# Causal attention and a gated MLP on one core: the score products of later pairs of heads in another number format

## The chip, the cores and the metric

The kernel runs on one core of one Trainium2 chip. The metric is the device time of one execution in microseconds. A core has a TensorE matrix engine (PE; its weight loads are listed apart as PEld), a vector engine (DVE), ScalarE (ACT), GpSimd (POOL) and SyncE (SP), whose queue issues all of this kernel's DMA transfers.

## What is computed

Causal attention over 4 batches of 12 heads (448 positions, 64 values a head), then a gated MLP over 768 channels with a mixing along the sequence. The reference, shortened:

```python
scores = q @ k.transpose(0, 1, 3, 2) / sqrt(64)
attn = softmax(where(causal, scores, -1e9))
x = (attn @ v).transpose(0, 2, 1, 3).reshape(4, 448, 768)
h = gelu_tanh(x @ w_in)
u, v = h[..., :512], h[..., 512:]
v_n = (v - mean(v)) / sqrt(var(v) + 1e-6) * g_ln
v_s = einsum('ts,bsd->btd', w_sg, v_n) + b_sg[None, :, None]
out = x + (u * v_s) @ w_out
```

All inputs and outputs are fp32.

## The kernel before

The work of a batch is six pairs of heads (24 pairs in all, `pair`, L475) and one MLP (`mlp`, L636). Two heads of a pair lie in the two halves of the 128 partitions, 64 rows each.

A pair loads q and k transposed, side by side, into one tile `qk` of 128x896 values (L481, L482; a pool of two such tiles). `score` (L485 to L491) multiplies them in fp32: four chunks of queries and keys (the table `CH`, L24), with 448, 64, 320 and 192 key columns, issued as two groups, (448, 64) and (320, 192). In each chunk the two heads stand one after the other in the code, on rows 0 to 63 and 64 to 127 of the array, into separate PSUM banks. The vector engine scales and masks the scores and takes the row minimum of the negated values (L503), ScalarE does exp with running sums (L511). The sums' reciprocals are transposed (L525), copied (L526), written to a scratch in memory (`rd`, L530) and read back as a broadcast tile `rb` (L533; two buffers, L524). TensorE transposes the probabilities (L542), ACT and DVE evict them into `ph` (L547, L549), `pv` multiplies them with v (L573), and DVE scales the result with `rb` into `xt` (L585). `keep_x` (L592) stores `xt` as the residual and splits it into a high part rounded to fp32r (L597 on POOL for batch 0, L599 on ACT later) and a low part, the difference (POOL, L600 and L602).

The MLP works with fp32r throughout: each product is the sum of three, high by high, high by low, low by high, with 128 rows of the array and 448 or 512 columns a matmul (`group`, L611 to L621, three matmuls of a group at a time). Its weights are split in the same way during the start (`split_w`, L407; `split_w64`, L420). The parts are: v half of the first product with GELU and normalisation (L646 to L688; the normalising step is L675), u half (L689), sequence mixing and gate (L702), output product (L730), which reads the residual from memory into `res` tiles of 128x2x448 (L737, L738, two buffers), adds it (L750) and stores the sums, two blocks of 128 channels together for batches 0 to 2 (L758) and singly for the last batch (L754).

The order is not that of the code. `Order` (L92) collects all steps with an engine, an estimated duration, their reads and writes and a priority (`at`), then places them one by one in a simulated schedule (`plan`, L136): on each engine, of the steps that are ready, the one with the lowest priority value goes first. Priorities come from `STEP`, `MLP` and `LEN` (L41 to L43) and from the offsets in `DUE` (L55). Durations are the estimates passed to `od.add`; they affect the order alone. A buffer's next use waits for all users of its previous one. Each engine runs its list in order, and a waiting step holds up all behind it; this holds for SP's transfers too.

Of the kernel before, what the change touches and what calls it, by code (L numbers as in the profile page):

```python
# [37 lines left out]
)  # L38
PW = 1024

STEP = [10.25, 12.58, 26.17, 15.7]  # L41
MLP = [-9.07, 44.62, 63.06, -36.56]
LEN = [120.74, 28.59, 116.13, 144.04]  # L43

EV = 10, 10, 10, 10

WARM, FILL, EARLY = 10, 0, 2

# [4 lines left out]
BANKS = dict(s=6, tx=1, ty=1, o=2, m=6)  # L53

DUE = dict(  # L55
    gb=-70.31, r=(-73.94, 167.17, -182.74, -112.01), load=(-22.24, -27.25, 21.84, 40.98),
    S=(-24.73, 16.46, -37.71, 59.93), mx=(-67.58, -177.74, -157.41, -61.27),
    ex=(-6.0, -124.31, 178.09, -22.45), inv=(-79.87, -84.21, -150.39, -0.57),
    Tr=(-30.25, -187.23, -175.59, 53.63), T=(-15.71, 12.99, -7.14, 20.55),
    ev=(-69.22, -68.97, -23.68, -241.47), V=(-34.92, 18.81, -178.88, -94.68),  # L60
    PV=(-7.79, -32.53, 14.54, 62.09), xo=(-147.05, 14.03, -41.95, -96.66),
    xs=(5.67, -159.72, 24.75, 158.69), post=(50.68, 88.74, -27.16, 37.5), wv=-22.34, wu=145.87,
    wo=100.49, mu=(6.77, 13.82, -8.74, 40.54), ms=(3.19, 41.66, -9.72, 72.98),
    mo=(-13.84, 150.66, 53.35, 188.48),
)
# [225 lines left out]
def attention_gated_mlp(ctx: ExitStack, tc: tile.TileContext, qk, vP, w_in, g_ln, w_sgT, b_sg, w_out, out):  # L291
# [53 lines left out]
    def dma(fn, r, w, at, size, early=0.0):  # L345
        od.add("sp", 0.48, fn, r, w, at, size=size / 330e3, early=early)
# [8 lines left out]
        od.add("dve", 0.068 + n * rate / 1000, fn, r, w, at, done, port=port)  # L355

    def pool_tt(n, fn, r, w, at):
        od.add("pool", 0.15 + n * 0.0021, fn, r, w, at, port=True)

    def start(p):  # L360
        b, h = divmod(p, HP)
# [58 lines left out]
    def split_w64(src, dst, key, n, at, pool_, tag, words, early=0.0):  # L420
        t = buf(pool_, tag, *words)
        it = lambda: t.t.bitcast(I32).rearrange("p a b -> p (a b)")[:, 0:2 * n].rearrange("p (n t) -> p n t", t=2)
        lo = lambda: it()[:, :, 0]
        hi = lambda: it()[:, :, 1]
        dma(lambda: nc.sync.dma_start(out=t.t.bitcast(I32).rearrange("p a b -> p (a b)")[:, 0:2 * n],
                                      in_=src.bitcast(I32)), [], [t], at - 6, n * 1024, early)
        kh, kl = (t, "hi"), (t, "lo")
        act(n, lambda: nc.scalar.activation(out=f(hi()), in_=f(hi()), func=AF.Prelu, scale=2.0 ** -112, alpha=2.0 ** 32),  # L428
            [t], [kh], at, True)
        dve(n, lambda: nc.vector.tensor_scalar(out=lo(), in0=lo(), scalar1=29, scalar2=None,  # L430
                                               op0=ALU.logical_shift_right), [t], [kl], at, 0.53, port=True)
        dve(n, lambda: nc.vector.scalar_tensor_tensor(out=lo(), in0=hi(), scalar=3, in1=lo(),
                                                      op0=ALU.logical_shift_left, op1=ALU.bitwise_or),
            [t, kh], [kl], at, port=True)
        od.add("pool", 0.13 + n * 0.0012, lambda: nc.gpsimd.tensor_copy(dst(0), f(lo())), [t, kl], [(key, 0)], at, port=True)
        pool_tt(n, lambda: nc.gpsimd.tensor_tensor(out=dst(1), in0=f(lo()), in1=f(dst(0)), op=ALU.subtract),
                [t, kl, (key, 0)], [(key, 1)], at)

# [9 lines left out]
    def weights_b():  # L448
        def load():
            nc.sync.dma_start(out=gcol, in_=g_ln)  # L450
            nc.sync.dma_start(out=bB, in_=bass.AP(tensor=b_sg.tensor, offset=b_sg.offset, ap=[[0, 128], [1, S]]))

        dma(load, [], ["gb"], 20, 229e3, LATER["g"])

        def halve():
            nc.vector.tensor_scalar(out=gcol, in0=gcol, scalar1=0.5, scalar2=None, op0=ALU.mult)
            nc.vector.tensor_scalar(out=bB, in0=bB, scalar1=0.5, scalar2=None, op0=ALU.mult)

        dve(512, halve, ["gb"], ["gb"], DUE["gb"])
# [15 lines left out]
    def pair(p):  # L475
# [2 lines left out]
        per = STEP[b]  # L478
        ib = [(2 * p + z) % NP for z in range(2)]
        s = [[bank("s") for k in range(2)] for z in range(2)]  # L480
        qk_ = buf(two, "qk", [128, 2, S])  # L481
        dma(lambda: nc.sync.dma_start(out=qk_.t, in_=qk[p]), [], [qk_], T + due("load", b), 459e3)  # L482


        def score(cs):  # L485
            for c in cs:
                m, n, bk, col, q0 = CH[c]
                for z in range(2):
                    r = slice(64 * z, 64 * z + 64)
                    nc.tensor.matmul(out=s[z][bk].t[:, col:col + n], lhsT=qk_.t[r, 0, q0:q0 + 128],  # L490
                                     rhs=qk_.t[r, 1, 0:n], start=True, stop=True)  # L491
        for cs in ((3, 0), (2, 1)):
            pe(sum(max(CH[c][1] * 4 / 2400, 0.214) + 0.01 for c in cs), lambda cs=cs: score(cs), [qk_],
               [s[z][CH[cs[0]][2]] for z in range(2)], T + due("S", b), (64, 128))


# [24 lines left out]
            nc.vector.tensor_reduce(out=tot, in_=sm[ip], op=ALU.add, axis=mybir.AxisListType.X)  # L521
            nc.vector.reciprocal(out=rs, in_=tot)
        od.add("dve", 0.3, inv, sk + ["sm"], ["rs"], T + due("inv", b))
        rb, sb = buf(two, "rb", [128, 512]), s[1][1]  # L524
        pe(0.12, lambda: nc.tensor.transpose(sb.t[0:8, 0:128], rs.rearrange("p z c -> p (z c)"), ident), ["rs", "ident"], [sb], T + due("Tr", b))  # L525
        dve(128, lambda: nc.vector.tensor_copy(rT[ip], sb.t[0:8, 0:128]), [sb], [("rT", ip)], T + due("inv", b))  # L526

# [64 lines left out]
    def keep_x(b, hp, x, To, Ty):  # L592
# [43 lines left out]
    def mlp(b):  # L636
# [93 lines left out]
        for mc in range(KC):  # L730
            ps = bank("m")
            at = step(2.27) + due("mo", b)
            d = slice(mc * 128, (mc + 1) * 128)
            z = mc % 2
            if z == 0:
                d2 = slice(mc * 128, (mc + 2) * 128)
                rr = buf(two, "res", [128, 2, S])  # L737
                dma(lambda rr=rr, d2=d2: nc.sync.dma_start(out=rr.t, in_=xd[b, d2, :].rearrange("(a p) s -> p a s", a=2)),  # L738
                    [("xd", b, mc), ("xd", b, mc + 1)], [rr], at - 6, 459e3)
            mms, r = [], []  # L740
            for c in range(FC):
                y = gT[c]
# [4 lines left out]

            cuts = ((0, S // 2), (S // 2, S)) if (b, mc) == (B - 1, KC - 1) else ((0, S),)
            for k, (lo, hi) in enumerate(cuts):
                dve(hi - lo, lambda rr=rr, ps=ps, z=z, lo=lo, hi=hi: nc.vector.tensor_tensor(  # L750
                    out=rr.t[:, z, lo:hi], in0=ps.t[:, lo:hi], in1=rr.t[:, z, lo:hi], op=ALU.add),
                    [ps, rr], [(rr, 2 * k + z)], at + 2.3 + due("post", b))
                if b == B - 1:
                    dma(lambda rr=rr, d=d, z=z, lo=lo, hi=hi: nc.sync.dma_start(out=out[b, d, lo:hi],  # L754
                                                                                in_=rr.t[:, z, lo:hi]),
                        [(rr, 2 * k + z)], [], at + 2.3, 512.0 * (hi - lo))
            if b < B - 1 and z:
                dma(lambda rr=rr, d2=d2: nc.sync.dma_start(out=out[b, d2, :].rearrange("(a p) s -> p a s", a=2),  # L758
                                                           in_=rr.t), [(rr, 0), (rr, 1)], [], at + 2.3, 459e3)
# [50 lines left out]
```

## Time and profile before

| | us |
|---|---|
| median of 3 runs (382.56 to 383.92) | 383.64 |
| profiled execution, its own time | 383.15 |
| its span, first to last instruction | 381.4 |
| PE busy | 372.1 |
| DVE busy | 255.3 |
| ACT busy | 211.8 |
| POOL busy | 146.6 |

The execution's own time is 1.75 us longer than the span. Busy time counts every stretch in which at least one instruction of the engine is under way; matmuls overlap, so a busy PE says that work is in its pipeline, not that it runs at its peak. A matmul's duration in the records contains a latency that the next one hides: the cost of one in a run is the distance between starts. An fp32 matmul of the code is recorded as two matmuls with two weight loads.

### The profile page before, as it was taken

What the parts mean: (1) busy time and instruction counts of PE and PEld (TensorE: products, weight loads), DVE (VectorE), ACT (ScalarE), POOL (GpSimd) and SP (SyncE); (2) the same over time, 40 slices, a digit from 0 to 9 for tenths busy, and PEclk for the clock granted to TensorE, in tenths of its full rate; (3) what the DMA queues carried; (4) which work ended last, traced back from release to release, by engine and by line L of the source; (5) the groups of instructions that cost most, each with busy time, mean ns of one, the idle gap of its engine ahead of it and who ended that gap; (6) DMA issues with size and microseconds to landing.
All of it is one profiled execution on the core that took longest, in us unless ns stands there. A gap on an engine that the chain in (4) does not pass through costs nothing.

```text
span 381.4 us, 6771 instructions
## 1 busy us (share of the span) xinstructions
PE 372.1 (98%) x2202; PEld 289.4 (76%) x2202; DVE 255.3 (67%) x812; ACT 211.8 (56%) x671; POOL 146.6 (38%) x171
## 2 busy tenths in 40 slices
PE   8789999999999999999999999999999999999996
PEld 3455675787778876787879778777877788889995
DVE  3999887899996497757756364376867652475422
ACT  2978855976966187694297234264875660343200
POOL 3355595947688210114034620013008611040530
PEclk9899999999999999999999999999999999999999
DMA  7579878736532486720313355341332235100044
GB/s 249 199 223 300 274 243 282 237 112 208 163 117 85 135 260 193 229 89 8 130 38 98 86 159 161 112 147 36 105 105 61 61 116 169 48 0 2 0 144 144
DMA packets 27602, 52.70 MB, mean 138 GB/s; under 512 B 2736, under 2 KB 15792, under 8 KB 27568
## 3 DMA queue, kind: packets, MB, share of 16 engines
q1 hardware_dynamic: 27568, 52.28, 43.5%
q8 instruction: 17, 0.28, 0.3%
q14 instruction: 17, 0.14, 0.1%
HBM read 39.68 MB, written 12.58 MB: 137 GB/s over the span
## 4 chain that ended last, share of the span: by engine, by line
PE 80%; DMA 10%; ACT 4%; DVE 3%; issue 1%; SPq 1%; POOL 0%; DVEq 0%; POOLq 0%
PE m L619 54%; PE o L573 9%; PE s L490 9%; DMA rb<-rd 4%; PE tx L542 4%; PE ty L542 4%; ACT P L511 3%; DMA rd<-rT 2%; DMA qk<-in_qk_dram 2%; DMA vraw<-in_vP_dram 1%; DVE s L503 1%; DVE xt L585 1%; ACT ph L549 1%; PE s L525 1%; ACT vn L428 0%
## 5 line engine op out<-in xcount | busy, mean ns | idle before, releaser
L511 ACT ACTIVATE P<-s,ngm 64x64 f32<-64x64 f32 (+3 forms) x240 | 99.9, 424 | 23.8 <-DVE ngm L503 22.0
L503 DVE CUSTOM_DVE_ANT_0 s<-s,mask 128x448 f32<-128x448 f32 (+2 forms) x192 | 75.2, 447 | 12.4 <-PE s L490 12.2
L619 PE MATMUL m<-win,x 128*128 128x512 f32 (+1 forms) x264 | 67.0, 402 | 0.8 <-POOL x L600 0.5
L619 PE MATMUL m<-x,win 128*128 128x448 f32 x288 | 63.8, 371 | 0.0
L619 PE MATMUL m<-gT,wout 128*128 128x448 f32 x288 | 63.2, 370 | 0.0
L619 PEld LDWEIGHTS m<-win,x 128*128 128x128 f32 (+1 forms) x264 | 46.8, 183 | 13.7 <-POOL x L600 0.9
L600 POOL TENSOR_TENSOR x<-xt,x 128x448 fp32r<-128x448 f32 x24 | 28.2, 1175 | 74.8 <-ACT x L599 74.3
L619 PEld LDWEIGHTS m<-gT,wout 128*128 128x128 f32 x288 | 52.6, 188 | 4.6 <-issue 0.4
L619 PEld LDWEIGHTS m<-x,win 128*128 128x128 f32 x288 | 52.4, 188 | 4.6 <-issue 0.5
L490 PE MATMUL s<-qk 64*128 64x64 f32 (+3 forms) x384 | 55.1, 408 | 0.3 <-DMA qk<-in_qk_dram 0.2
L490 PEld LDWEIGHTS s<-qk 64*128 64x128 f32 x384 | 33.1, 188 | 22.5 <-issue 13.7
L573 PE MATMUL o<-ph,vraw 128*64 128x448 f32 (+3 forms) x384 | 48.6, 387 | 0.9 <-DVE xt L585 0.7
L511 ACT ACTIVATION_READ_ACCUMULATOR P<-s,ngm 128x1 f32 (+1 forms) x240 | 47.2, 197 | 0.0
L549 ACT ACTIVATE ph<-tx 128x512 f32<-128x512 f32 x48 | 28.5, 594 | 29.4 <-PE tx L542 27.5
L573 PEld LDWEIGHTS o<-ph,vraw 128*64 128x64 f32 x384 | 25.7, 137 | 25.1 <-issue 13.6
L547 DVE COPY ph<-ty 128x512 f32<-128x512 f32 x48 | 32.8, 683 | 11.2 <-PE ty L542 10.9
L619 PE MATMUL m<-wsg,vn 128*128 128x448 f32 x176 | 39.2, 372 | 0.0
L673 POOL TENSOR_TENSOR mv<-mv,mhalf 128x1 f32<-128x1 f32 (+1 forms) x16 | 8.8, 552 | 68.3 <-DVE mv L671 68.2
L619 PEld LDWEIGHTS m<-wsg,vn 128*128 128x128 f32 x176 | 32.2, 188 | 3.2 <-issue 0.2
L628 DVE SCALAR_TENSOR_TENSOR tmp<-tmp,m 128x448 f32<-128x448 f32 (+1 forms) x28 | 17.9, 641 | 21.8 <-ACT tmp L627 21.7
L627 ACT ACTIVATE tmp<-m 128x448 f32<-128x448 f32 (+1 forms) x28 | 15.7, 565 | 30.1 <-PE m L619 29.3
L542 PE MATMUL tx<-ident,P 128*128 128x128 f32 x144 | 30.1, 280 | 1.6 <-ACT P L511 1.3
(75 smaller groups left out, 468.4 us busy)
## 6 DMA issues: line engine op xcount, KB each, us to landing
qk<-in_qk_dram SPq DMA_DIRECT2D x24, 448.0 KB
vn<-in_w_in_dram SPq DMA_DIRECT2D x12, 512.0 KB
vraw<-in_vP_dram SPq DMA_DIRECT2D x24, 256.0 KB
rb<-rd SPq DMA_DIRECT2D x24, 256.0 KB
xd<-xt SPq DMA_DIRECT2D x24, 224.0 KB
res<-xd SPq DMA_DIRECT2D x12, 448.0 KB
out_dram<-res SPq DMA_DIRECT2D x9, 448.0 KB
gT<-in_w_out_dram SPq DMA_DIRECT2D x8, 384.0 KB
```

Source lines behind the costliest of these rows:

```text
L490: nc.tensor.matmul(out=s[z][bk].t[:, col:col + n], lhsT=qk_.t[r, 0, q0:q0 + 128], rhs=qk_.t[r, 1, 0:n], start=True, stop=True)
L503: nc.vector.tensor_tensor_reduce(out=o, in0=o, in1=mk, scale=-0.125, scalar=3e38, op0=ALU.add, op1=ALU.min, accum_out=ngm[ib[z]][c][0:m])
L511: act(n, lambda c=c, m=m, r0=r0, k0=k0, n=n, bk=bk, col=col, off=off, kc=kc, i=i, z=z: nc.scalar.activation(out=P[i][r0:m, off:off + n], i ...
L542: nc.tensor.transpose(out, P[i][:, col:col + 128], idn)
L547: dve(512, lambda: nc.vector.tensor_copy(pT[z][k].t, tz.t), [tz], [pT[z][k]], Te)
L549: act(512, lambda: nc.scalar.activation(out=pT[z][k].t, in_=tz.t, func=AF.Copy), [tz], [pT[z][k]], Te)
L573: nc.tensor.matmul(out=o.t[r, q0:S], lhsT=vr.t[0:n, c, r], rhs=pT[z][k].t[0:n, lo:hi], start=(c == 0), stop=(c == 3))
L600: pool_tt(S, lambda: nc.gpsimd.tensor_tensor(out=y.t[:, S + 64:], in0=x.t, in1=f(y.t)[:, 0:S], op=ALU.subtract), [x, y], [(y, 1)], Ty)
L619: nc.tensor.matmul(out=ps.t[0:l().shape[1], 0:n], lhsT=l(), rhs=rr(), start=(k == 0), stop=(k == len(mms) - 1))
L627: act(n, lambda: nc.scalar.activation(out=z(), in_=h(), func=AF.Square), [ps], [t], at)
L628: dve(n, lambda: nc.vector.scalar_tensor_tensor(out=z(), in0=z(), scalar=1.0 / GC, in1=h(), op0=ALU.add, op1=ALU.mult), [ps], [t], at)
L673: od.add("pool", 0.46, lambda mv=mv, m=m: nc.gpsimd.tensor_tensor(out=mv.t[0:m, 1:2], in0=mv.t[0:m, 1:2], in1=mhalf[0:m], op=ALU.pow), ["s ...
```

## The change

From pair 10 on (`WHOLE`), q and k are split on chip. A high part rounded to fp32r is made by ACT in batches 0 and 1 (`QH`) and by POOL in batches 2 and 3, so by ACT for pairs 10 and 11; the low part is the difference, made by POOL. The scores are then the sum of three fp32r products, high by high, high by low and low by high, accumulated in PSUM, with the two heads in turn inside each product. Pairs 0 to 9 keep their fp32 products. The loaded tile, the high and the low part share one pool of three slots; `rb` has one buffer in place of two. The residual in the MLP is loaded, and the result stored, in single blocks of 128 channels with three buffers. The priorities (`STEP`, `MLP`, `LEN`, `DUE`, `LATER`) and several of the planner's duration estimates have other values.

```diff
-STEP = [10.25, 12.58, 26.17, 15.7]
-MLP = [-9.07, 44.62, 63.06, -36.56]
-LEN = [120.74, 28.59, 116.13, 144.04]
+STEP = [0.35, 18.93, 53.33, 18.75]
+MLP = [32.49, 93.72, 57.46, -13.84]
+LEN = [127.46, 38.01, 117.31, 115.0]
...
+QH = [1, 1, 0, 0]
+
+WHOLE = 10
...
-        od.add("pool", 0.15 + n * 0.0021, fn, r, w, at, port=True)
+        od.add("pool", 0.15 + n * 0.00224, fn, r, w, at, port=True)
...
-        qk_ = buf(two, "qk", [128, 2, S])
+        qk_ = buf(three, "qk", [128, 2, S])
         dma(lambda: nc.sync.dma_start(out=qk_.t, in_=qk[p]), [], [qk_], T + due("load", b), 459e3)
+        if p < WHOLE:
+            side, rq = (lambda l: qk_.t), [qk_]
+            parts, cost = ((0, 0),), lambda n: max(n * 4 / 2400 + 0.036, 0.245)
+        else:
+            qh, ql = (buf(three, "qk", [128, 2, S], F32R) for l in range(2))
+            if QH[b]:
+                act(2 * S, lambda: nc.scalar.activation(out=qh.t, in_=qk_.t, func=AF.Copy), [qk_], [qh], T + due("qh", b), True)
+            else:
+                od.add("pool", 0.13 + 2 * S * 0.00105, lambda: nc.gpsimd.tensor_copy(qh.t, qk_.t), [qk_], [qh],
+                       T + due("qh", b), port=True)
+            pool_tt(2 * S, lambda: nc.gpsimd.tensor_tensor(out=ql.t, in0=qk_.t, in1=f(qh.t), op=ALU.subtract),
+                    [qk_, qh], [ql], T + due("ql", b))
+            side, rq = (lambda l: ql.t if l else qh.t), [qh, ql]
+            parts, cost = ((0, 0), (0, 1), (1, 0)), lambda n: 3 * max(n / 2400 + 0.017, 0.06)
...
                 m, n, bk, col, q0 = CH[c]
-                for z in range(2):
-                    r = slice(64 * z, 64 * z + 64)
-                    nc.tensor.matmul(out=s[z][bk].t[:, col:col + n], lhsT=qk_.t[r, 0, q0:q0 + 128],
-                                     rhs=qk_.t[r, 1, 0:n], start=True, stop=True)
+                for k, (a, l) in enumerate(parts):
+                    for z in range(2):
+                        r = slice(64 * z, 64 * z + 64)
+                        nc.tensor.matmul(out=s[z][bk].t[:, col:col + n], lhsT=side(a)[r, 0, q0:q0 + 128],
+                                         rhs=side(l)[r, 1, 0:n], start=(k == 0), stop=(k == len(parts) - 1))
...
-        rb, sb = buf(two, "rb", [128, 512]), s[1][1]
+        rb, sb = buf(one, "rb", [128, 512]), s[1][1]
...
-        per = n / 2400 + 0.0155
+        per = n / 2400 + (0.02 if n == 512 else 0.0135)
...
-            z = mc % 2
-            if z == 0:
-                d2 = slice(mc * 128, (mc + 2) * 128)
-                rr = buf(two, "res", [128, 2, S])
...
+            rr = buf(three, "res", [128, S])
+            dma(lambda rr=rr, d=d: nc.sync.dma_start(out=rr.t, in_=xd[b, d, :]), [("xd", b, mc)], [rr], at - 6, 229e3)
...
+                dma(lambda rr=rr, d=d, lo=lo, hi=hi: nc.sync.dma_start(out=out[b, d, lo:hi], in_=rr.t[:, lo:hi]),
+                    [(rr, k)], [], at + 2.3, 512.0 * (hi - lo))
```

## Rows read from the trace of the kernel before

**Rows 1.** The page's busy shares and granted TensorE clock in 40 slices.

```profile
PE 372.1 (98%) x2202; PEld 289.4 (76%) x2202; DVE 255.3 (67%) x812; ACT 211.8 (56%) x671; POOL 146.6 (38%) x171
...
PEclk9899999999999999999999999999999999999999
```

**Rows 2.** Stretches: PE, PEld, DVE, ACT, POOL busy us (instructions); granted clock; DMA share, GB/s.

```profile
20.00:30.00 10.00, 8.93 (x70) 5.96 (x67) 9.14 (x40) 6.85 (x27) 6.03 (x6) 1.00 0.81 256
70.00:100.00 30.00, 30.00 (x188) 23.19 (x187) 27.79 (x85) 24.01 (x73) 21.30 (x23) 1.00 0.56 174
140.00:160.00 20.00, 19.86 (x141) 14.00 (x139) 15.07 (x69) 15.86 (x65) 2.07 (x4) 1.00 0.65 207
```

**Rows 3.** The chain that ended last: start us, length us, what it passes through.

```profile
22.95 4.52 DMA rb<-rd
...
57.14 6.67 DMA rb<-rd
...
66.56 4.00 PE m L619 x16
...
75.99 0.61 PE m L619 x3
...
111.95 2.04 PE s L490 x16
...
302.09 2.04 PE s L490 x16
...
316.00 61.89 PE m L619 x296
```

**Rows 4.** Score records around 226 us: ns min/median/max, first and last start.

```profile
L490 PE MATMUL s<-qk x4: 536/588/640, 225.2 to 225.7; 64*128 64x448 f32 x4
...
L490 PE MATMUL s<-qk x6: 216/272/536, 225.7 to 226.1; 64*128 64x64 f32 x4, 64*128 64x448 f32 x2
L490 PEld LDWEIGHTS s<-qk x2: 187/187/187, 226.0 to 226.1; 64*128 64x128 f32 x2
```

**Rows 5.** Weight loads (PEld) in order of time: start us, us, count.

```profile
225.19 0.30 PEld L490 LDWEIGHTS s<-qk 64*128 64x128 f32 x4
...
225.67 0.19 PEld L490 LDWEIGHTS s<-qk 64*128 64x128 f32 x2 [0.18 <-issue]
...
226.04 0.30 PEld L490 LDWEIGHTS s<-qk 64*128 64x128 f32 x4 [0.18 <-issue]
...
227.22 0.30 PEld L619 LDWEIGHTS m<-gT,wout 128*128 128x128 f32 x2 [0.23 <-issue]
```

**Rows 6.** The page's groups: matmuls of the MLP's last part and their weight loads.

```profile
L619 PE MATMUL m<-gT,wout 128*128 128x448 f32 x288 | 63.2, 370 | 0.0
...
L619 PEld LDWEIGHTS m<-gT,wout 128*128 128x128 f32 x288 | 52.6, 188 | 4.6 <-issue 0.4
```

**Rows 7.** Groups by shape on GpSimd and ScalarE; DVE's L675 at 75 to 90 us.

```profile
L600 POOL TENSOR_TENSOR x<-xt,x 128x448 fp32r<-128x448 f32 x24 | 28.2, 1175 | 74.8 <-ACT x L599 74.3
...
L602 POOL TENSOR_TENSOR x<-xt,x 128x64 fp32r<-128x64 f32 x24 | 8.8, 367 | 0.0
...
L597 POOL CAST x<-xt 128x448 fp32r<-128x448 f32 x6 | 3.5, 589 | 4.9 <-DVE xt L585 4.9
...
L599 ACT ACTIVATE x<-xt 128x448 fp32r<-128x448 f32 x18 | 10.4, 575 | 13.7 <-DVE xt L585 13.6
...
L675 DVE TENSOR_SCALAR tmp<-tmp,mv x3: 529/1001/1387, 79.6 to 87.3; 128x512 f32<-128x512 f32 x3
```

**Rows 8.** SP's waits before 66 us; broadcast issues; the scaling at 27 us.

```profile
SPq L482 <- PE s L490: 10.6, 4, 4.7
...
26.14 0.52 SPq L533 DMA_DIRECT2D rb<-rd  x1
...
L533 SPq DMA_DIRECT2D rb<-rd x4: 518/518/519, 37.0 to 57.1; - x4
...
27.49 0.75 DVE L585 TENSOR_TENSOR xt<-o,rb 128x256 f32<-128x256 f32 x3 [0.54 <-DMA rb<-rd]
```

More of the change, by code (lines that the diff above doesn't have):

```diff
@@ L55 @@
 DUE = dict(
[L56 to L64, printed above, removed]
-)
-LATER = dict(u=-7.46, g=51.07, s=56.43, o=66.41)
-TICK, BUSY, SHIFT = 10.24 / 3, 3400, 0.1
+    gb=-151.71, r=(-150.61, 385.44, -233.89, -54.33), load=(-74.94, 97.74, 291.03, 24.74),
+    qh=(-67.79, 56.53, -115.4, 13.09), ql=(-167.6, -128.07, -126.51, 153.75),
+    S=(26.71, 37.52, -44.26, 113.92), mx=(-128.36, -163.44, -261.85, -177.48),
+    ex=(-26.64, -154.57, 233.74, -153.21), inv=(-12.46, -237.64, -276.87, -209.76),
+    Tr=(-38.31, -119.16, -260.92, -68.85), T=(13.28, -75.93, -144.0, 15.27),
+    ev=(-31.26, -137.17, 57.15, -62.37), V=(-97.84, 10.47, -316.62, -221.69),
+    PV=(-88.85, -41.68, 3.17, -15.08), xo=(-168.6, -61.12, 139.72, -60.85),
+    xs=(84.2, -178.57, 79.78, 4.5), post=(-37.35, 81.95, -87.51, -6.62), wv=-32.52, wu=-23.93,
+    wo=146.89, mu=(0.74, 35.17, 9.84, 106.16), ms=(11.49, 102.99, 71.11, 144.23),
+    mo=(4.12, 199.81, 152.83, 149.18),
+)
+LATER = dict(u=-210.2, g=61.23, s=51.42, o=72.37)
+TICK, BUSY, SHIFT = 10.24 / 3, 3400, 0.09
 COLD = 6.0, 1.8
@@ L434, in split_w64 @@
             [t, kh], [kl], at, port=True)
-        od.add("pool", 0.13 + n * 0.0012, lambda: nc.gpsimd.tensor_copy(dst(0), f(lo())), [t, kl], [(key, 0)], at, port=True)
+        od.add("pool", 0.13 + n * 0.00105, lambda: nc.gpsimd.tensor_copy(dst(0), f(lo())), [t, kl], [(key, 0)], at, port=True)
         pool_tt(n, lambda: nc.gpsimd.tensor_tensor(out=dst(1), in0=f(lo()), in1=f(dst(0)), op=ALU.subtract),
@@ L451, in load @@
             nc.sync.dma_start(out=bB, in_=bass.AP(tensor=b_sg.tensor, offset=b_sg.offset, ap=[[0, 128], [1, S]]))
-        dma(load, [], ["gb"], 20, 229e3, LATER["g"])
+        dma(load, [], ["gb"], 20, 459e3, LATER["g"])
         def halve():
@@ L487, in score @@
                 m, n, bk, col, q0 = CH[c]
-                for z in range(2):
-                    r = slice(64 * z, 64 * z + 64)
-                    nc.tensor.matmul(out=s[z][bk].t[:, col:col + n], lhsT=qk_.t[r, 0, q0:q0 + 128],
-                                     rhs=qk_.t[r, 1, 0:n], start=True, stop=True)
+                for k, (a, l) in enumerate(parts):
[3 more added lines that the diff above has]
+                                         rhs=side(l)[r, 1, 0:n], start=(k == 0), stop=(k == len(parts) - 1))
         for cs in ((3, 0), (2, 1)):
-            pe(sum(max(CH[c][1] * 4 / 2400, 0.214) + 0.01 for c in cs), lambda cs=cs: score(cs), [qk_],
+            pe(sum(cost(CH[c][1]) for c in cs), lambda cs=cs: score(cs), rq,
                [s[z][CH[cs[0]][2]] for z in range(2)], T + due("S", b), (64, 128))
@@ L596, in keep_x @@
         if b == 0:
-            od.add("pool", 0.13 + S * 0.0012, lambda: nc.gpsimd.tensor_copy(y.t[:, 0:S], x.t), [x], [y], Ty, port=True)
+            od.add("pool", 0.13 + S * 0.00105, lambda: nc.gpsimd.tensor_copy(y.t[:, 0:S], x.t), [x], [y], Ty, port=True)
         else:
@@ L733, in mlp @@
             d = slice(mc * 128, (mc + 1) * 128)
-            z = mc % 2
-            if z == 0:
-                d2 = slice(mc * 128, (mc + 2) * 128)
-                rr = buf(two, "res", [128, 2, S])
-                dma(lambda rr=rr, d2=d2: nc.sync.dma_start(out=rr.t, in_=xd[b, d2, :].rearrange("(a p) s -> p a s", a=2)),
-                    [("xd", b, mc), ("xd", b, mc + 1)], [rr], at - 6, 459e3)
+            rr = buf(three, "res", [128, S])
+            dma(lambda rr=rr, d=d: nc.sync.dma_start(out=rr.t, in_=xd[b, d, :]), [("xd", b, mc)], [rr], at - 6, 229e3)
             mms, r = [], []
@@ L749, in mlp @@
             for k, (lo, hi) in enumerate(cuts):
[L750 to L759, printed above, removed]
+                dve(hi - lo, lambda rr=rr, ps=ps, lo=lo, hi=hi: nc.vector.tensor_tensor(
+                    out=rr.t[:, lo:hi], in0=ps.t[:, lo:hi], in1=rr.t[:, lo:hi], op=ALU.add),
+                    [ps, rr], [(rr, k)], at + 2.3 + due("post", b))
+                dma(lambda rr=rr, d=d, lo=lo, hi=hi: nc.sync.dma_start(out=out[b, d, lo:hi], in_=rr.t[:, lo:hi]),
+                    [(rr, k)], [], at + 2.3, 512.0 * (hi - lo))
     weights_a()
```

## The prediction

> **What bounds the kernel now.** I read the page's busy shares first: TensorE is busy 98% of the span, its granted clock at the upper of its two levels (2.4 GHz) in all but an early slice, the vector, scalar and GpSimd engines far lower [rows 1]. A share is an average over stages, so the stretches come next: from 70 us on TensorE has no idle time to speak of (30.00 of 30, 19.86 of 20), while at 20 to 30 us it is idle for about a tenth [rows 2]. The chain in order of time says the same. Before 66 us it passes through the normaliser's transfers, each 4.5 to 6.7 us long; afterwards it is TensorE's matmuls one behind the other, ending in 296 matmuls of the MLP over 61.89 us [rows 3]. So the kernel has two stages: a start set by transfers and softmax, and a long stage where a microsecond less of TensorE's own work is a microsecond less of time. All 14 pairs that change lie in the second: pair 10's set stands at 111.95 us, the last one ends at 304 us [rows 3].
>
> **What one set of scores costs now.** One pair (two heads, four chunks of 448, 64, 320 and 192 columns) takes 2.04 us [rows 3]. Each fp32 product is recorded as two matmuls, a high and a low half of the weights, so 16 records a pair. The steady one of 448 columns lasts 536 ns, that of 64 columns 216 ns [rows 4]: 0.833 ns a column, two passes at 2.4 GHz. The two heads start together and share the time. Streaming: 2 x 0.833 x (448 + 320 + 192) = 1.60 us. The 64-column products are different: the second weight loads of a pair begin about 0.11 us after the first (0.30 against 0.19 us for the group, twice [rows 5]), and the 64-column low half lasts 272 ns (the median of its row) where its high half lasts 216, so it waited 56 ns for its weights [rows 4]. A slot shorter than 0.11 us is filled up to that by its weight load: two such slots, 0.22 us. The remaining 0.22 us is entering the 64-row arrangement and the first exposed load.
>
> **The new set.** Three products (high-high, high-low, low-high) replace one fp32 product, 24 matmuls a pair in place of 16 records, each with its own load. (Nothing here drops a repeated load: in the MLP the same weights stand in two matmuls running, and loads and matmuls are equally many, 288 and 288 [rows 6].) An fp32r matmul of 448 columns costs 0.203 us (0.61 for three [rows 3]): one pass, 0.187, and about 0.016 more. The loads keep their 0.11 us: the MLP's fp32r loads take 188 ns each, as those of the scores do at 187 [rows 4, 6], and its second one also begins 0.11 us after the first [rows 5]. Two heads side by side, I take:
> 448 columns, 3 x 0.203 = 0.61; 64 columns, load-bound, 3 x 0.11 = 0.33; 320 columns, 3 x (0.133 + 0.016) = 0.45; 192 columns, two slots load-bound at 0.11 and one of 0.096, 0.32; entering, 0.22 as before. The sum is 1.93 against 2.04, **0.11 us a pair, 1.5 us for 14 pairs**. The change trims 1.60 us of streaming to about 1.3 and gives much of it back as waits for weights.
> No row shows an fp32r matmul under 448 columns, so this is bounded from both sides. If loads never bind, 64 columns cost 3 x 0.043 and 192 columns 3 x 0.096: 1.70 us, a gain of 4.8 us in all. If the narrow streams (192, 64) run at fp32's whole pace, twice 0.16 us and twice 0.11 us per product: 3 x 0.32 + 3 x 0.22 in place of 0.65, 2.90 us, a loss of 12 us. I take the load-bound value because the 112-ns spacing is measured on the same 128 weight columns.
>
> **The splits.** From pair 10 each pair adds a rounding copy and a subtraction of 128x896. The subtraction goes by GpSimd's rows (64 columns 367 ns, 448 columns 1175 ns [rows 7]): 1175 + 448 x 2.1 ns = 2.1 us. The copy is twice the 589 ns row, 1.2 us; for pairs 10 and 11 ScalarE does it, about 1.0 us from its 575 ns. GpSimd gains 14 x 2.1 + 12 x 1.2 = 44 us on 147, still about half of the span, and has 18 of 20 us free at 140 to 160 [rows 1, 2]. I cost this at nothing: TensorE has MLP groups to run meanwhile. If that cover is gone, scores wait about 3.7 us behind their load (copy, subtraction, handoffs). The vector engine pays a little: beside a busy GpSimd one of its 0.53 us normalisations took 1.39 [rows 7]; that is off the chain.
>
> **The buffers.** Loaded pair, high and low part share three slots. Up to pair 9 that is a third slot for the load: in the first 66 us the transfer queue stood four times, 10.6 us in all, on a load whose slot the scores still held, with everything queued behind it [rows 8]. The normaliser's buffer goes from two to one: the second broadcast is issued at 26.14, the first product that reads its predecessor's at 27.49 for 0.75 [rows 8], so it would stand 2.1 us; the last four are issued between 37.0 and 57.1, 6.7 us apart on the mean [rows 8], and fit. Net I estimate one mean wait less in the start, 10.6 / 4 less part of that 2.1: **1.0 us gained**, bounds one broadcast either way (-4.5 to +4.5).
> The residual's transfers are cut in two (12 loads become 24, nine paired stores 18, same bytes): some 21 more issues of 0.3 to 0.5 us on a queue that mostly waits. The stores of the last batch were single already, so the tail of 62 us is unchanged: nothing. The retuned due times and planner prices reorder ready work; as TensorE is always fed after 66 us they can only change how often it changes arrangement (about 0.2 us each, as on entering a score set): nothing, within 1 us either way.
>
> **Sum.** 383.15 us (the profiled execution: span 381.4 and 1.75 around it) - 1.5 - 1.0 = 380.65. That execution stood 0.5 under the median of 383.64, so I give 380.9. A measurement of this kernel tells about 0.5%, 1.9 us, from no change: faster is below 381.7, slower above 385.6.
>
> **Rivals.**
> (1) *Loads do not bind in fp32r.* For: the 320-column streams cover them anyway, and rows show the wait only at 64 columns in fp32. 383.6 - 4.8 - 1.0 = 377.8. Chance 0.20.
> (2) *Narrow fp32r streams are no faster than fp32.* For: none under 448 columns is on record. Against: fp32's own passes keep 0.833 ns a column from 64 to 448. It decides once the 192-column trio takes over 0.65 us. 383.6 + 12 - 1.0 = 394.6; if only the 192-column ones slow, 14 x (0.96 - 0.32) = 9.0 above the forecast, 390. Slower. Chance 0.10.
> (3) *Weights no longer load beneath a stream of the same rows.* The low-half loads of the first chunk all ended at 225.49 beneath 448-column streams that ran until 225.67 and beyond [rows 4, 5], which speaks against. It would expose 0.107 us before each of 12 slots: 3 x (0.43 + 4 x 0.107) + 0.1 = 2.7 us, 9 us more in all: 392. Chance 0.03. The Trainium skill ("TensorE: Matmul & The Clock Gate", Part 3, The mechanism) says that a weight load overlaps a matmul in flight only when its row group differs; by that rule this rival would hold, and the trace disagrees, with loads 0.11 us apart beneath one stream.
> (4) *The split comes late.* One set of slots means that the next high part waits for the last scores, and 3.7 us pass before the next scores can run; where pairs stand closer and the MLP offers nothing, TensorE idles. For: GpSimd's queue is in order and holds the MLP's normalisation too (21.30 of 30 us busy at 70 to 100 [rows 2]). Against: from 111.95 to 302.09 there are 14 sets, 14.6 us apart on the mean [rows 3]. Two or three such stops: 383.6 - 2.5 + 5 = 386. Chance 0.13.
> (5) *Nothing moves*, since the start keeps its length and the loads give back all: 383.6. Chance 0.09.
>
> **How the numbers follow.** My forecast holds 0.45, its own range 378.5 to 383.5: 0.29 faster, 0.14 same, 0.02 slower. Rival 1 adds 0.19 faster and 0.01 same, rival 4 0.02 faster, 0.03 same and 0.08 slower, rival 5 0.02, 0.06 and 0.01, rivals 2 and 3 0.13 slower. Together 0.52, 0.24 and 0.24. The range reaches from a load-free set with a start 3 us shorter, 375, to 388, past rival 4; left out are rivals 2 and 3 and a little below.
>
> **What would show it.** Score matmuls of pairs from 10 on should appear as 24 records, 336 in all. Right: a set of about 1.9 us, 64-column records starting 0.11 us apart, 192-column ones too, 448 at 0.20. Rival 1 shows 0.04 to 0.06 and sets near 1.7; rival 2 shows 192-column records over 0.2 apart; rival 3 gaps before each record; rival 4 shows weight loads of the scores waiting for GpSimd. The start is right if the first full run of MLP matmuls begins about 1 us before 66.56 [rows 3]. A stop of TensorE over 1 us after 70 us, or a start moved by more than 4 us, would make the prediction wrong whatever the set costs.

## The result and the profile after

The changed kernel took 387.49 us (median of 4 runs, 387.13 to 387.99), the kernel before 383.15 on the same chip: ratio 1.0113, interval 1.0087 to 1.0138. It is 4.3 us slower where I forecast 2.7 faster. Measured again later, it was 385.84 against 382.82, ratio 1.0061 [1.0024, 1.0098] (e9 below): slower again, by about half as much.

The page's busy shares and the granted clock in 40 slices, of the changed kernel, which answer to [rows 1]:

```profile
PE 373.8 (97%) x2314; PEld 299.0 (78%) x2314; DVE 257.5 (67%) x812; ACT 215.4 (56%) x673; POOL 186.9 (48%) x197
...
PEclk9699799999999999999999999999999999999999
```

GpSimd has its 40 us more (146.6 before) and the weight loads, more in number, their 9.6 (289.4 before); nothing else on this line moved by more than 4. What changed stands in the second line: two dips of the granted clock, in the second and the fifth slice, where before there was one shallow one. The stretches, with the columns of [rows 2], show the same place:

```profile
10.00:20.00 10.00, 6.81 (x25) 4.70 (x25) 6.67 (x31) 9.89 (x43) 0.00 (x0) 0.66 0.41 164
20.00:30.00 10.00, 9.31 (x67) 6.12 (x66) 9.19 (x34) 9.06 (x30) 5.95 (x6) 1.00 0.49 143
30.00:40.00 10.00, 8.59 (x50) 5.74 (x52) 7.69 (x34) 6.63 (x24) 4.21 (x5) 0.84 0.90 275
40.00:50.00 10.00, 10.00 (x61) 6.01 (x63) 7.66 (x30) 7.04 (x29) 6.27 (x8) 0.82 0.75 229
```

At 20 to 30 us the transfers moved 143 GB/s where [rows 2] has 256, and at 40 to 50 us TensorE is busy all the time, but over a third of it at the lower clock (granted 0.82 on the mean): busy is not work done. The chain of the changed kernel, with the columns of [rows 3]:

```profile
67.43 5.27 DMA tmp<-in_w_sgT_dram
...
84.55 7.30 PE m L639 x33
...
160.23 1.90 PE s L510 x24
...
261.92 1.90 PE s L510 x24
...
291.78 1.89 PE s L510 x24
...
324.56 57.09 PE m L639 x272
```

The sets of scores from pair 10 on take 1.90 us in place of 2.04. But a transfer still stands in the chain at 67 us, and the first full run of MLP matmuls comes at 84.55, where [rows 3] has one at 66.56. Not all of these 18 us are delay: e13 below, whose start loses no more than that of the kernel before, has the same run of 33 at 78.84.

**How much is lost where.** Busy time can't tell this, so I count work. Each matmul record is given what its shape costs in a steady run at the upper clock, taken as the distance between starts (0.201 us for fp32r with 448 columns, 0.232 with 512, 0.109 for a transpose of 128; a pair of two fp32r heads side by side 0.201, 0.149, 0.11 and 0.11 a product for 448, 320, 192 and 64 columns). The time that passed less that sum is TensorE's lost time: idle, waiting for weights, or at the lower clock. It is worked out from the records of one profiled execution each.

| lost time, us | up to 50 us | up to 90 us | from 90 us on | whole |
|---|---|---|---|---|
| before | 18.2 | 22.4 | 12.3 | 34.7 |
| after | 21.9 | 27.1 | 12.8 | 39.9 |

The steady work itself (the span less the lost time) fell by 1.2 us, from 346.7 to 345.5. So the whole loss, and more, stands before 90 us: 4.7 us, ahead of pair 10, where no changed score is computed yet.

**What is late there.** SP's instructions in order of time (start, length, line, transfer; a first waiting issue is part of the length), first of the kernel before:

```profile
8.66 2.63 SPq L482 DMA_DIRECT2D qk<-in_qk_dram  x2
14.25 0.33 SPq L425 DMA_DIRECT2D vn<-in_w_in_dram  x1
15.94 0.63 SPq L530 DMA_DIRECT2D rd<-rT  x2
...
22.95 0.85 SPq L533 DMA_DIRECT2D rb<-rd  x1
```

and of the changed kernel, with its wait before 66 us (total, times, longest) as [rows 8] has it:

```profile
8.08 14.27 SPq L487 DMA_DIRECT2D qk<-in_qk_dram  x3
23.68 0.33 SPq L430 DMA_DIRECT2D vn<-in_w_in_dram  x1
24.72 0.64 SPq L550 DMA_DIRECT2D rd<-rT  x2
...
29.05 0.60 SPq L553 DMA_DIRECT2D rb<-rd  x1
```
```profile
SPq L487 <- PE s L510: 18.1, 4, 11.7
```

The third slot didn't relieve the queue here. Six loads of q and k now stand ahead of w_in's fourth tile, where four did, so the queue stands on pair 5's load, 11.7 us at once until pair 2's scores are done, and w_in's fourth tile and the first normaliser come 9 us later than before. The engines' lists changed with it: the exponentials of pairs 0 and 1 now go ahead of w_in's unpacking, whose first step on ScalarE begins at 19.4 us (before 7.4). GpSimd has nothing to do at 10 to 20 us, 3.94 us before.

### The profile page after: what moved, and what is told of

It is laid out like the page before. It is cut to its first block, busy times and chain, and to the rows that moved or that the text cites. A ratio compares the mean times of both kernels' runs of the same rounds, so it can differ in the third digit from the quotient of the medians.

```text
span 385.4 us, 7034 instructions
## 1 busy us (share of the span) xinstructions
PE 373.8 (97%) x2314; PEld 299.0 (78%) x2314; DVE 257.5 (67%) x812; ACT 215.4 (56%) x673; POOL 186.9 (48%) x197
## 4 chain that ended last, share of the span: by engine, by line
PE 89%; DMA 4%; DVE 2%; ACT 2%; issue 1%; SPq 0%; DVEq 0%; POOL 0%; ACTq 0%
PE m L639 55%; PE o L593 11%; PE s L510 10%; PE tx L562 6%; PE ty L562 5%; DMA vn<-in_w_in_dram 2%; DMA tmp<-in_w_sgT_dram 1%; DMA vraw<-in_vP_dram 1%; ACT P L531 1%; DVE s L523 1%; PE m L407 1%; PE s L545 1%; ACT ph L569 0%; DVE ph L567 0%; ACT vn L433 0%
## 5 line engine op out<-in xcount | busy, mean ns | idle before, releaser
L639 PE MATMUL m<-gT,wout 128*128 128x448 f32 x288 | 64.2, 371 | 0.0
L639 PE MATMUL m<-x,win 128*128 128x448 f32 x288 | 61.0, 367 | 0.0
L639 PEld LDWEIGHTS m<-x,win 128*128 128x128 f32 x288 | 53.2, 188 | 4.4 <-issue 0.2
L510 PE MATMUL s<-qk 64*128 64x448 f32 (+2 forms) x496 | 55.1, 347 | 1.5 <-DVE xt L605 1.3
L639 PEld LDWEIGHTS m<-win,x 128*128 128x128 f32 (+1 forms) x264 | 46.9, 183 | 12.3 <-issue 0.2
L510 PEld LDWEIGHTS s<-qk 64*128 64x128 f32 x496 | 40.6, 189 | 17.8 <-issue 9.0
L620 POOL TENSOR_TENSOR x<-xt,x 128x448 fp32r<-128x448 f32 x24 | 28.5, 1189 | 43.2 <-ACT x L619 42.6
L531 ACT ACTIVATION_READ_ACCUMULATOR P<-s,ngm 128x1 f32 (+1 forms) x240 | 48.1, 200 | 0.0
L593 PEld LDWEIGHTS o<-ph,vraw 128*64 128x64 f32 x384 | 26.6, 140 | 26.2 <-issue 14.9
L567 DVE COPY ph<-ty 128x512 f32<-128x512 f32 x48 | 32.8, 682 | 12.3 <-PE ty L562 10.2
L639 PE MATMUL m<-wsg,vn 128*128 128x448 f32 x176 | 40.4, 375 | 0.0
L562 PE MATMUL tx<-ident,P 128*128 128x128 f32 x144 | 31.4, 289 | 3.7 <-issue 2.0
L648 DVE SCALAR_TENSOR_TENSOR tmp<-tmp,m 128x448 f32<-128x448 f32 (+1 forms) x28 | 17.9, 644 | 23.5 <-ACT tmp L647 23.4
L605 DVE TENSOR_TENSOR xt<-o,rb 128x256 f32<-128x256 f32 (+2 forms) x72 | 18.0, 305 | 21.4 <-DMA rb<-rd 13.6
```

The lines of the kernel that those rows point to most:

```text
L510: nc.tensor.matmul(out=s[z][bk].t[:, col:col + n], lhsT=side(a)[r, 0, q0:q0 + 128], rhs=side(l)[r, 1, 0:n], start=(k == 0), stop=(k == len ...
L531: act(n, lambda c=c, m=m, r0=r0, k0=k0, n=n, bk=bk, col=col, off=off, kc=kc, i=i, z=z: nc.scalar.activation(out=P[i][r0:m, off:off + n], i ...
L562: nc.tensor.transpose(out, P[i][:, col:col + 128], idn)
L567: dve(512, lambda: nc.vector.tensor_copy(pT[z][k].t, tz.t), [tz], [pT[z][k]], Te)
L593: nc.tensor.matmul(out=o.t[r, q0:S], lhsT=vr.t[0:n, c, r], rhs=pT[z][k].t[0:n, lo:hi], start=(c == 0), stop=(c == 3))
L605: nc.vector.tensor_tensor(out=two_(x.t, a[0]), in0=two_(o.t, a[0]), in1=two_(rb.t, a[1]), op=ALU.mult)
```

## The experiments

Many of these kernels hold a fixed order: the planner's call is replaced by a list of step numbers, so that one thing can be changed without planning everything anew.

```diff
-        for n in self.plan():
+        for n in ORDER:
```

The ratios are to the kernel before on the same chip; they are not the quotients of the two medians.

| run | us, median | ratio to before [interval] | lost up to 90 us / whole |
|---|---|---|---|
| e1 | 391.03 | 1.0190 [1.0148, 1.0233] | 28.8 / 45.0 |
| e2 | 388.97 | 1.0155 [1.0107, 1.0203] | 22.5 / 39.7 |
| e3 | 387.33 | 1.0111 [1.0078, 1.0144] | 24.1 / 38.5 |
| e4 | 390.83 | 1.0218 [1.0178, 1.0257] | 28.3 / 43.4 |
| e5 | 387.57 | 1.0165 [1.0118, 1.0212] | 25.1 / 38.7 |
| e6 | 397.80 | 1.0408 [1.0382, 1.0435] | 22.0 / 49.8 |
| e7 | 410.31 | 1.0737 [1.0700, 1.0774] | 23.8 / 63.1 |
| e8 | 388.93 | 1.0155 [1.0101, 1.0209] | 29.4 / 42.6 |
| e9 | 385.84 | 1.0061 [1.0024, 1.0098] | 28.1 / 40.9 |
| e10 | 398.45 | 1.0415 [1.0376, 1.0454] | 37.4 / 51.6 |
| e11 | 386.10 | 1.0086 [1.0056, 1.0115] | 25.5 / 38.8 |
| e12 | 383.00 | 1.0008 [0.9976, 1.0039] | 22.4 / 34.7 |
| e13 | 383.82 | 1.0006 [0.9986, 1.0026] | 21.9 / 34.2 |
| e14 | 383.22 | 1.0010 [0.9983, 1.0038] | 23.5 / 36.3 |
| e15 | 383.40 | 1.0006 [0.9985, 1.0027] | not read |
| e16 | 385.09 | 1.0050 [1.0025, 1.0074] | 24.9 / 38.5 |
| e17 | 383.49 | 1.0005 [0.9988, 1.0022] | 22.1 / 35.7 |
| e18 | 386.86 | 1.0097 [1.0061, 1.0133] | 26.9 / 40.2 |

### Parts of the change, planned anew

e1 drops the split and keeps all else, e2 gives the changed kernel the priorities of the kernel before, e3 gives the kernel before a single `rb`, e4 bars the loads of pairs 3 to 5 before 16, 21 and 27 us.

```diff
-WHOLE = 10
+WHOLE = 24
```
```diff
-STEP = [0.35, 18.93, 53.33, 18.75]
-MLP = [32.49, 93.72, 57.46, -13.84]
+STEP = [10.25, 12.58, 26.17, 15.7]
+MLP = [-9.07, 44.62, 63.06, -36.56]
...
```
```diff
-        rb, sb = buf(two, "rb", [128, 512]), s[1][1]
+        rb, sb = buf(one, "rb", [128, 512]), s[1][1]
```
```diff
-        dma(lambda: nc.sync.dma_start(out=qk_.t, in_=qk[p]), [], [qk_], T + due("load", b), 459e3)
+        dma(lambda: nc.sync.dma_start(out=qk_.t, in_=qk[p]), [], [qk_], T + due("load", b), 459e3, {3: 16.0, 4: 21.0, 5: 27.0}.get(p, 0.0))
```

> The changed kernel with WHOLE = 24: all 24 pairs keep fp32 scores, no split anywhere; buffers, residual blocks and numbers of the change stay. Theory (the start was lengthened by the order of the transfers, the split itself gains 0.14 us a pair, 1.90 against 2.04): the start loses what it loses in the changed kernel and 14 x 0.14 = 1.9 us come on top, 389.4 us. Rival (the split, with its 44 us more of GpSimd work and its later scores, is what costs): 383 to 385 us.

> The changed kernel with STEP, MLP, LEN, DUE and LATER of the kernel before (qh and ql 20 us ahead of the scores' own offset); split, three slots, one rb buffer and single residual blocks stay. Theory (order): 381 to 382.5 us, 383.2 less 1.9, with the transfer queue standing under 5 us at a time in the start. Rival (split or buffers cost): 385.5 us or more.

> The kernel before with one rb buffer in place of two and nothing else. Theory (order): 383 to 384 us, no more than one wait of 2.1 us in the start, and that partly hidden. Rival (the single rb buffer is what lengthened the start): 386 us or more.

> The changed kernel; the q and k loads of pairs 3, 4 and 5 get an earliest planned time (16, 21 and 27 us), which moves pair 5's load behind the loads and copies that stand behind it now in SP's queue. Theory (SP stood 11.7 us on that load, and w_in and the normaliser's copies came late): 383 to 385 us, the stop of 11.7 us gone, the second stretch at the lower clock gone. Rival (split or buffers cost): 387 to 388 us, unchanged.

All four came out 387 to 391 us. e1 has no split at all, and its start loses 28.8 us: the split is not what slows the start. e2 has the start of the kernel before (22.5 us lost) but loses 9.1 us at 90 to 160, where that kernel loses 5.3. In e4 the long wait only changed hands, to a load of w_in, 11.6 us until the vector engine had unpacked an earlier tile. And e3, which costs 4.2 us here, costs nothing in e12, with the same buffer and the order kept but for nine broadcasts:

```diff
-        rb, sb = buf(two, "rb", [128, 512]), s[1][1]
+        rb, sb = buf(one, "rb", [128, 512]), s[1][1]
...
-        for n in self.plan():
+        for n in ORDER:
```

> The kernel before with one rb buffer, its own order of steps written out: nine of the 24 broadcasts stand 5 to 79 places later, where the one buffer is free. Theory (the 4 us of e3_one_rb came from planning anew, not from waiting for the buffer): within 1.5 us of the kernel before. Rival (the wait for the one buffer costs): 3 us or more over it.

So planning anew is itself worth some 4 us for this small edit, and runs that plan anew price a part badly. From here on the order is fixed.

### One order, other contents; other orders, same contents

e5 is the changed kernel's order with fp32 scores in all pairs; its split steps are empty. e6 is the changed kernel's code in the order of the kernel before (13 of 1912 steps had to move), e7 the same with two `rb` and two `res` buffers.

```diff
...
+            od.add("act" if QH[b] else "pool", 1.0, lambda: None, [qk_], [qh], T)
+            od.add("pool", 2.0, lambda: None, [qk_, qh], [ql], T)
...
-            side, rq = (lambda l: ql.t if l else qh.t), [qh, ql]
-            parts, cost = ((0, 0), (0, 1), (1, 0)), lambda n: 3 * max(n / 2400 + 0.017, 0.06)
+            side, rq = (lambda l: qk_.t), [qk_, qh, ql]
+            parts, cost = ((0, 0),), lambda n: n
```

> The changed kernel with its own order of steps written out, in which the split steps of the 14 pairs are empty and their scores are fp32 again; nothing is re-planned. Theory (the split gains 0.14 us a pair on TensorE and its GpSimd work is hidden): 387.5 + 1.9 = 389.4 us. Rival (the split costs): 387 us or less.

> The changed kernel (split, three slots, one rb buffer, single residual blocks) in the order of the kernel before, as far as the buffers let it: 13 of 1912 steps stand over 20 places later, nine loads of q and k and four broadcasts. Theory A (the new order of the steps costs 4 to 5 us in the start): 381.5 to 383 us. Theory B (the single rb buffer costs, as it did in the kernel before with one rb buffer, 4 us): 385.5 us or more.

> As e6_old_order_new_buffers with two rb buffers, and two in place of three residual blocks to make room. Theory A: 381.3 us, 383.2 less 14 x 0.14. Theory B: also 381.3, 4 us below e6_old_order_new_buffers. Rival (the split or its shared slots cost): 383 us or more.

e5 stands 0.5% above the changed kernel by the two ratios, 2 us, as the 0.14 us a pair would have it; the intervals overlap, so this leans and doesn't prove. e6 splits the question in two. Its start, with the changed kernel's buffers, loses 22.0 us, not 27.1: the buffers are not what slows the start. But from 90 to 200 us it loses 22.3 us, the changed kernel 6.2. Waits of SP and GpSimd in e6 at 66 to 200 us (total, times, longest):

```profile
SPq L573 <- POOL qk L584: 22.1, 6, 7.4
```
```profile
POOL qk L582 <- PE s L596: 18.7, 3, 7.9
```

Loads stand for slots that the split holds, and GpSimd stands for scores to free a slot. What TensorE waited for in the same stretch:

```profile
PE o L679 <- DMA vraw<-in_vP_dram: 8.1, 2, 4.3
PE s L596 <- POOL qk L584: 1.7, 1, 1.7
PE s L596 <- POOL qk L582: 1.1, 1, 1.1
```

So the stop of my rival 4 occurs here, but scores wait for the split for only 2.8 us; products wait for v for 8.1, and the rest of the loss is not traced to a wait of TensorE. The old order has no room for the split; the changed kernel's order has. e7 is 12.5 us slower still: with two residual blocks SP stood 57.0 us on stores (35.9 in e6), and it tells no more.

### Single steps moved

In the changed kernel's order, e8 puts the unpacking of w_in's first three tiles and the loads of the next three back to their old places and delays pair 5's load; e11 puts back the normaliser of pairs 0 to 5; e10 takes over the old order for the first batch's attention, w_in and the mixing weights as a whole. e9 is the changed kernel unedited.

> The changed kernel in its own order, but the unpacking of the first three w_in tiles (ScalarE, VectorE and GpSimd steps), the next three w_in loads and pair 5's load stand where the kernel before has them. Theory A (w_in's three staging tiles and the q and k slots are all held until 20 us, so that no transfer can be issued for 10 us): DMA share at 10 to 30 us back to 0.6 or more, 3 to 4 us of the start back, 383.5 to 385 us. Rival (the order of the start does not matter, the buffers or the split do): 387 to 388 us.

> The changed kernel once more, unedited, on the chip of the three runs below, to compare them with: 1.011 times the kernel before.

> The changed kernel with all its buffers and its split; the steps of batch 0's six pairs, of w_in and the loads of pairs 6 to 8 take the order of the kernel before, the rest keeps its own. Theory (the new order of the start costs 4.7 us, and nothing else is lost): TensorE's lost time at 90 us back from 27.1 to 22 to 23 us, one stretch of 3.4 us at the lower clock, 4 to 5 us under the changed kernel, 0.985 to 1.000 times the kernel before. Rival (one rb buffer or the split costs): within 1.5 us of the changed kernel.

> The changed kernel in its own order, but the five steps of the normaliser (sum and reciprocal, transpose, copy, two transfers) of pairs 0 to 5 stand where the kernel before has them, where that is earlier. Theory (it is this chain that is late: rT of pair 0 at 24.4 us where it was at 15.6, rb at 29.1 for 22.9, the scaling at 34.6 for 27.5): the scaling of pair 0 by 30 us, the stretch at the lower clock from 36.7 us gone, 3 to 5 us under the changed kernel. Rival (the unpacking of w_in or the bandwidth of the start is late as well): under 2 us.

e8 failed: nothing came back. e11 lost 1.6 us less up to 90 us than the changed kernel, and its ratio, 1.0086, is not under that of e9, 1.0061, on the same chip. e10 has the old start up to 50 us (18.6 us lost, 18.2 before) and then falls apart, since steps of the two orders mixed later stand in each other's way (one load stood 24.6 us). It can't price the start. e9 gave a spread: 383.69 to 389.98 in 10 runs.

### The old start, then the new order

The clean cut: all steps that the kernel before begins in its planner's first 20, 40 or 50 us stand first, in its order; all others follow in the changed kernel's order. Code, split and buffers are the changed kernel's.

> The changed kernel with its buffers and its split; the 91 steps that the kernel before begins in its planner's first 20 us stand first, in that kernel's order, and all others follow in the changed kernel's order. Theory (the new order of the whole start costs, step by step): a fifth of the start is put back, so 384 to 386 us, TensorE's lost time up to 90 us at 25 to 26 us (27.1 in the changed kernel, 22.4 in the kernel before). Rival (one early step decides, the load that stands for its slot or the late unpacking of w_in): all of it comes back here already, 382 us and 22 to 23 us lost. Rival (the late start is not what costs): 385.8 to 387.5 us as the changed kernel.

> As e13_start_20 with the 235 steps of the first 40 us. Theory (the order of the start costs 4.7 us and the split gains 1.4): lost time up to 90 us at 22 to 24 us, one stretch of 3 to 4 us at TensorE's lower clock in place of two of 6.8, and 382 to 383.5 us. Rival (an order that was planned for another start loses afterwards what it wins in the start): lost time up to 90 us at 22 to 24 us, but more than 14 us lost after it, and 385 us or more.

> As e13_start_20 with the 305 steps of the first 50 us. Theory: 381.5 to 383 us, the lost time up to 90 us at 22 to 23 us. Rival (loses afterwards what it wins in the start): 385 us or more with more than 14 us lost after 90 us.

Ninety-one steps are enough: with 20 us put back the ratio falls from 1.0061 to 1.0113 for the changed kernel to 1.0006, and 40 or 50 us add nothing. The first rival of e13 is right in place (it all comes back in the first 20 us), though not in size: 383.8, not 382. Engine by engine few steps differ: e13's lists are the changed kernel's with 23 steps moved, five of SP, three of TensorE, five of ScalarE and ten of the vector engine. e13's page, stretches, and the run of the MLP from its chain:

```profile
PEclk9999999999999999999999999999999999999999
```
```profile
10.00:20.00 10.00, 7.52 (x47) 3.90 (x43) 9.20 (x30) 9.02 (x38) 4.95 (x6) 1.00 0.52 185
20.00:30.00 10.00, 8.02 (x66) 5.42 (x64) 7.83 (x36) 8.56 (x31) 0.95 (x1) 1.00 0.64 195
30.00:40.00 10.00, 9.35 (x73) 6.17 (x69) 9.13 (x35) 9.05 (x36) 6.69 (x9) 1.00 0.80 251
40.00:50.00 10.00, 10.00 (x74) 7.46 (x71) 9.44 (x31) 7.56 (x29) 6.47 (x8) 1.00 0.97 337
```
```profile
78.84 7.29 PE m L725 x33
```

The clock stays at its upper level, and at 40 to 50 us a busy TensorE now runs 74 matmuls, where the changed kernel ran 61. At 20 to 30 us its transfers move 195 GB/s, between the changed kernel's 143 and the 256 of [rows 2], and yet all the lost time is back: their rate there doesn't decide. (e15's trace caught the longest of its executions, 388.12, and isn't read.)

Three kinds of moves lie in those 91 steps: SP's queue, what the computing engines do first, and the loads of pairs 1 and 2 ahead of w_in. e16 puts back all but SP's queue, e17 all but the two loads, e18 the two loads alone.

> As e13_start_20, but SP's queue alone keeps the changed kernel's order (the loads of q and k of the first six pairs ahead of the fourth tile of w_in and of the first normaliser); TensorE, ScalarE, VectorE and GpSimd have the order of e13_start_20. Theory A (what costs is what the engines do first: exponentials of two pairs ahead of w_in's unpacking and of the normaliser): 382.5 to 384 us, as e13_start_20. Theory B (what costs is SP's queue: q and k of pair 5 stand for a slot and all behind them come late): 385.5 to 388 us, as the changed kernel, with SP standing 10 us or more.

> As e13_start_20, but the loads of pairs 1 and 2 stand ahead of the first tile of w_in, as in the changed kernel, and nothing else is moved. If those two loads, 0.9 MB, hold up the first tiles of w_in and so the start: 385 to 387 us; if they don't: 383 to 384 us.

> The changed kernel, all engines in its order, with two steps moved: the loads of pair 1 behind the first tile of w_in and of pair 2 behind the first values, as the kernel before has them. If these two loads in front are what costs: 382.5 to 384 us; if the coupling of the engines' order and SP's queue is: 385.5 to 388 us, as the changed kernel.

The two loads cost nothing: e17 is at 1.0005 with them in front, e18 at 1.0097 with them put back. These two ran on one chip, and their intervals lie well apart. e16 lies between both theories at 1.0050. Its SP waits before 66 us and two stretches:

```profile
SPq L573 <- PE s L596: 18.1, 4, 11.2
```
```profile
10.00:20.00 10.00, 6.95 (x33) 3.78 (x29) 9.11 (x34) 9.95 (x40) 3.75 (x4) 0.83 0.41 158
20.00:30.00 10.00, 8.04 (x65) 5.76 (x66) 7.42 (x31) 7.67 (x31) 2.14 (x3) 1.00 0.57 184
```

The queue stands as in the changed kernel, 11.2 us at once, and the transfers move a little less than in e13, but GpSimd and VectorE are at work at 10 to 20 us, and one dip of the clock is left in place of two. By the ratios SP's queue costs 0.45% (e16 against e17), 1.7 us, and the engines' order the rest up to e18's 1.0097, 0.47%, 1.8 us. The intervals of e16 and e17 only just part and those of e16 and e18 overlap, so the halves are rough; what is shown is that putting the engines back doesn't give all of it. A step put back on one side waits for the other, as e4 showed.

## Why the prediction was wrong

**The new set: right, and a little more.** 1.90 us against the 1.93 I took; 14 x 0.14 = 2.0 us by the chain, 1.2 by the steady spacings, where I wrote 1.5. The load-bound reading holds for the set as a whole, though not slot by slot. In the set at 261.92, products of 64 columns start at 262.562, 262.593, 262.701, and the next one 0.112 us after: one short slot of 0.031, then 0.108 and 0.112, as far apart as their weight loads. In return the first of 320 columns takes 0.230, the others 0.149. Those of 192 columns take 0.084, 0.114 and 0.20 at the exit, the first of 448 takes 0.31 on entering. By chunks that is 0.72, 0.25, 0.53 and 0.40, where I had 0.61, 0.33, 0.45, 0.32 and 0.22 for entering: a sum that fits better than its terms. Rivals 1 and 2 fall with it, and so does rival 3: 24 loads of 0.18 to 0.19 us stand in a set of 1.90 us, which they could not if each had to wait for the streams to end.

**The splits: right.** GpSimd's and ScalarE's groups of the changed kernel, with the columns of [rows 7]:

```profile
L498 POOL TENSOR_TENSOR qk<-qk 128x896 fp32r<-128x896 f32 x14 | 29.6, 2118 | 0.8
...
L496 POOL CAST qk<-qk 128x896 fp32r<-128x896 f32 x12 | 11.2, 934 | 31.1 <-PE s L510 22.9 <-PE m L639 4.7 <-issue 3.5
```
```profile
L494 ACT ACTIVATE qk<-qk 128x896 fp32r<-128x896 f32 x2 | 1.9, 948 | 0.2 <-PE s L510 0.2
```

2.1 us as taken for the subtraction, 0.93 in place of 1.2 for the copy. After 90 us the view of TensorE's waits has no row in either kernel, so the splits are hidden, and rival 4 doesn't occur in the changed kernel. It does in e6, without the new priorities. e13, with the splits and the single residual blocks, loses 12.3 us after 90 us, as the kernel before: both cost nothing there, as I wrote.

**The buffers: too much expected.** I gave the third slot 1.0 us, from a queue that stood 10.6 us. In the changed kernel it stood 18.1. The slot alone is not to blame: with the old priorities (e2, first) or the old start (e13, second) the queue stands less than before.

```profile
SPq L487 <- PE s L510: 6.8, 3, 3.7
SPq L573 <- PE s L596: 8.4, 4, 3.2
```

It was the new priorities that filled the slot with loads put ahead. But the shorter waits bought next to nothing either: e2 and e13 lose 22.5 and 21.9 us up to 90 us, the kernel before 22.4. The single `rb` costs nothing (e12), less than the part of 2.1 us I set against the gain.

**The retuned numbers: this step failed.** I wrote "nothing, within 1 us either way", because TensorE is always fed after 66 us. That argued for one stage and was applied to all: priorities order the start too, where the chain runs through transfers and softmax. There they cost 4.7 us of TensorE's time in the profiled executions, shown by e13, where the old order of 91 steps alone takes the slowdown away. Nor could the old ones simply stay: with them the split costs later (e6; and e2, which loses 9.1 us at 90 to 160 where the kernel before loses 5.3).

With the measured terms the sum is 383.15 - 1.2 of steady work + 4.7 in the start + 0.5 after 90 us = 387.15, and the profiled execution took 387.13. This says where the time went and tests nothing, since lost time is what the work leaves of the span. Of my signs, the start moved by more than 4 us was the one that decided; the first full run of the MLP was a poor one, as e13 shows. That 387.49 lies inside my range of 375 to 388 is luck: its upper end was drawn for rival 4, which did not occur.

**What stays open.** e13, e14, e15 and e17 hold the split and the old start and only equal the kernel before; 1.2 to 2.0 us less was to be expected. e13's profiled execution has it (381.45 against 383.15, 0.5 us less lost), but only two of its 12 executions lie near 381.4, the others at 382.9 to 384.7, and the kernel before has one of 381.44 on the same chip: the gain of the split is not shown in the whole time. In e14 and e17 0.5 and 1.3 us of it are given back after 90 us. What differs between executions was not settled. No kernel beat the one before by more than its interval.

## What to carry to other kernels

When a change comes with new priorities, compare every engine's list, SP's first, in the stage where transfers set the end, and cost the moved steps there, even if the code that changed runs only later. An extra buffer on an in-order queue shortens a wait only if nothing is moved ahead to fill it. To price a part of such a change, fix the order first: planning anew alone moved this kernel by 4 us (e3 against e12).

## What the runs showed of the hardware

**The granted clock fell where TensorE had been idle in part.** In the changed kernel it went to the lower level twice. Stretches ahead of the two dips and inside them (columns as in [rows 2]):

```profile
10.00:12.80 2.80, 0.30 (x1) 0.14 (x1) 2.80 (x17) 2.79 (x12) 0.00 (x0) 1.00 1.03 416
...
33.00:36.70 3.70, 2.32 (x15) 1.23 (x15) 2.50 (x7) 2.62 (x9) 1.17 (x2) 1.00 0.92 340
```
```profile
13.00:19.50 6.50, 6.01 (x21) 4.22 (x22) 3.65 (x15) 6.40 (x31) 0.00 (x0) 0.50 0.15 59
...
37.00:43.50 6.50, 6.50 (x28) 3.68 (x26) 5.43 (x23) 5.48 (x22) 5.92 (x9) 0.50 0.80 242
```

0.50 is 1.2 GHz. TensorE was busy 0.30 of 2.8 us before the first dip and 2.32 of 3.7 before the second, then fully busy at half pace. The two dips last 13.6 us together, against 3.4 in the kernel before (14.0 to 17.4 us). The 10.2 us more cost up to 5.1 us of work (an estimate: half of them), about the size of the whole loss, though idle time and dips come together and no run separates them. In e13, busy 1.10 of 2 us at 10 to 12 and 1.52 of 2 at 12 to 14, there was no dip, so these rows don't say what decides it.

**The time was uneven with it.** The mean granted clock of single executions was 0.981 to 0.991 for the changed kernel over the 10 runs of e9, with times of 383.69 to 389.98, and 0.989 to 1.0 for the kernel before on the same chip, with 381.76 to 386.61; e13's was 0.996 to 1.0. Within e9 the three executions at 0.981 and 0.982 took 388.19 to 389.98, the others 383.69 to 387.15. That the clock makes the spread is not shown: e13's times spread from 381.39 to 384.70 at nearly one clock. The four runs of the result (387.13 to 387.99) showed less of the spread than these ten.
